# Delta-rule attention and a routed expert layer: other pairs of block inversions, masks and factors multiplied by GpSimd

## The chip, the cores and the metric

The kernel runs on one core of a Trainium2 chip. The metric is device time in microseconds from launch to end. Its engines run beside each other, each with an instruction queue of its own that is worked off in order: PE multiplies matrices, DVE and ACT compute elementwise, POOL (GpSimd) does so more slowly and also starts the indirect transfers, and SP starts most other transfers. SBUF is the on-chip memory; PE writes its results to PSUM, which DVE and ACT can read.

## The reference

Two blocks follow each other. The first is a delta-rule recurrence over 768 tokens, for 4 batches and 8 heads with 48 columns each; the second routes each of the 3072 tokens to 2 of 8 experts with two layers each.

```python
k_n = k / (norm(k) + 1e-6)
for t in range(S):                              # S = 768
    y[t] = q[t] @ state                         # per batch and head, 48 x 48
    v_old = k_n[t] @ state
    state = state + beta[t] * outer(k_n[t], v[t] - v_old)
x = y laid out as (B * S, H * D)                # 3072 x 384

noisy = x @ w_gate + log1p(exp(x @ w_noise)) * noise
top2, weights = the two largest of 8 experts, softmax over them
for each expert e and its tokens:
    out[token] += weight * (relu(x @ w1[e]) @ w2[e])    # 384 -> 1024 -> 384
```

All is in float32.

## The kernel before

**Units and steps.** The recurrence is worked in chunks of 64 tokens. A *unit* is one chunk of two batches (all 8 heads, 128 partitions); there are 12 chunks times 2 pairs of batches, so 24 units. A *step* is two chunks, hence four units; there are 6 steps, 0 to 5, and step s holds units 4s to 4s + 3.

**Products of keys and inversions.** Within a chunk the recurrence is the solution of a triangular system. `products(n)` turns the keys of a unit on PE, multiplies them with each other and copies the blocks of 32x32 into a tile `t` of `inverses`. `invert(g)` inverts all blocks of a group of steps at once on DVE: a transpose, the lengths and factors (with a logarithm and an exponential on ACT), and then 30 columns `j`, each of which is a multiply (line 828) and an add (line 832) that read two operands in SBUF. `GROUPS` says which steps are inverted together: a group of two steps makes each of these 60 operations twice as long. For each step `turn_back` then multiplies the tile with `lower`, a triangle of factors that GpSimd cuts out, and with -1 (line 848), and transposes it twice (lines 855 and 863) to `tb` and `tt`. `INVERTED_AT` and `KEYS_AT` are the places of the tiles.

**Joining and solving.** `join` copies the inverses of 32x32 from `tt` to `w64` on ACT (line 891; eight copies of the last step on DVE) and makes inverses of 64x64 of them with PE products that ACT copies out (lines 925 to 932, with a factor -1 on the way). `recur(n, ...)` is one unit of the recurrence: GpSimd multiplies v with the norms (line 995), PE multiplies keys with queries and with the state, DVE subtracts the second from v (line 1021) and multiplies the first with the causal `mask` (line 1028), PE solves for u, ACT copies u (line 1057), PE adds to the state and ACT copies it (line 1084). `answer` makes y from the masked product `qk`, u and the state; the products with `qk` are issued together with the solve of the following unit where both lie in one group of steps (`PAIRED`), and by themselves at the end of a group.

**Routing.** After steps 1, 3 and 5 `route(g)` takes the two largest experts of the tokens of two steps, counts, and gives each token its two rows in `rows_x`. Sixteen indirect transfers by GpSimd (line 420, called spreads here) write the rows, each held back until PE has reached a certain product, and kept apart by `SPACED` in the plan, save for the last routing. The rows of `rows_x` have to be cleared before (`clear`, `clear_more`): these transfers hang on columns of step 0 and of step 1. `early(1)` and `early(3)` load the first four tiles of expert 0 (line 1406) and work them with the lowest priority.

**Order.** None of this order is that of the text. Each operation is a job with an engine, a cost in us and the data it reads and writes. `Jobs.order` plays through all engines with these costs and picks, among the jobs that can start within `PATIENCE`, the one with the earliest due time. The due times are the constants `BEGINS`, `ENDS`, `ROUTED`, `STORED`; `SOON` pulls in the jobs of a PSUM bank once it is opened, and `COLD` stretches PE's costs by step. The result is written out as it is: every engine's queue has a fixed order.

**Experts.** The rest of expert 0 (line 1888) and the experts 1 to 7 (line 1744) follow, in an order written by hand, with sums of blocks on DVE and GpSimd that save products. Nothing here is touched.

Of the kernel before, what the change touches and what calls it, by code (L numbers as in the profile page):

```python
# [12 lines left out]
ALU = mybir.AluOpType  # L13
# [4 lines left out]
C = 64  # L18
# [6 lines left out]
ROW = 384 + 4  # L25

ROUTES = [(0, 2), (2, 2), (4, 2)]
GROUPS = [(0,), (1, 2), (3, 4), (5,)]
INVERTED_AT = [(0, 0), (1, 0), (0, 0), (1, 0)]
KEYS_AT = [0, 1, 3, 2, 0, 1]  # L30


BEGINS = [1.5, 48.2, 117.9, 200.0]
ENDS = [42.6, 117.5, 132.8, 196.9, 235.5, 240.6]
ROUTED = [146.3, 235.6, 329.3]
STORED = [205.2, 290.3, 366.8]
SOON = 6.93
SPACED = 3.3
COLD = [1.5, 1.35, 1.25, 1.15, 1.1, 1.05]
COLD_KEYS = [1.4, 1.4, 1.3, 1.2, 1.1, 1.1]  # L40

# [56 lines left out]
class Jobs:  # L100
# [145 lines left out]
                    could[jobs[j].engine].add(j)  # L246
        return sorted(done, key=lambda job: job.start)

    PATIENCE = 0.299

    def run(self, link):

# [11 lines left out]
def kernel(  # L264
# [39 lines left out]
    nc = tc.nc  # L304
# [6 lines left out]
    NS = NCH // 2  # L311
    NU = B // 2
    US = 2 * NU
# [17 lines left out]
        out=mask_u, in_=mask_u, pattern=[[1, 128]], base=0, channel_multiplier=-1,  # L331
# [137 lines left out]
    def deltanet(ictx):  # L469
# [5 lines left out]
        jobs = Jobs([psum.tile([128, 2, 512], FP32, name=f"pair{i}") for i in range(3)])  # L475
        p_st = psum.tile([128, 2, 512], FP32, name="p_st")
        PE, ACT, DVE, POOL, SP = Jobs.ENGINES
# [30 lines left out]
        def two_banks(p, cols):  # L508

            return p.tile[:, :, 0 : NP * cols].rearrange("p z (j d) -> p z j d", d=cols)  # L510
# [6 lines left out]
        NQ, N_U = 2 * NU, 3 * NU  # L517
# [207 lines left out]
        def invert(g):  # L725
# [115 lines left out]
            def turn_back(i):  # L841
                s, half = group[i], halves_of[i]
                ends, y, t_key = ENDS[s], inverses[held_in][:, half], ("t", held_in, half)
                if i:
                    only_lower(i)
                jobs.add(
                    DVE, 1.22,
                    lambda y=y: v_.scalar_tensor_tensor(
                        out=y, in0=y, scalar=-1.0, in1=lower, op0=ALU.mult, op1=ALU.mult
                    ),  # L850
                    reads=["lower"], writes=[t_key], due=ends - 4.0,
                )
                jobs.add(
                    DVE, 1.95,
                    lambda y=y: v_.transpose(
                        out=tbs.rearrange("p h j -> p j h"),
                        in_=y.rearrange("p i j -> p j i"),
                    ),
                    reads=[t_key], writes=["tb"], due=ends - 2.0,
                )  # L860
                jobs.add(
                    DVE, 1.95,
                    lambda y=y: v_.transpose(
                        out=tts.rearrange("p h i -> p i h"), in_=y
                    ),
                    reads=[t_key], writes=["tt", ("free", held_in, half)], due=ends,
                )
# [3 lines left out]
        def join(units):  # L871

            pairs = [(slice(lo, lo + Q), slice(lo + Q, lo + 2 * Q)) for lo in (0, C)]

            def part_of(t, n):
                i = n % US
                return t[:, i * H : (i + 1) * H]  # L880

            for n in units:
                w64, tt = w64s(n), part_of(tts, n)
                for lo in range(0, 128, Q):
                    rows, cols = slice(lo, lo + Q), slice(lo % C, lo % C + Q)
                    on, copy = (DVE, nc.vector.tensor_copy) if n >= US * (NS - 1) and lo % C else (
                        ACT, nc.scalar.copy
                    )
                    jobs.add(
                        on, 0.4,  # L890
                        lambda rows=rows, cols=cols, w64=w64, tt=tt, copy=copy: copy(  # L891
                            w64[rows, :, cols], tt[rows]
                        ),
                        reads=["tt"], writes=[("w", n % NW, lo)],
                    )
            for n, m in zip([*units, None], [None, *units]):
                p = bank(1)
                reads = []
                if n is not None:
                    reads += ["tb", ("at", slot_of(n))]  # L900
                if m is not None:
                    reads += [("x", m % 2), *(("w", m % NW, lo) for lo in (Q, C + Q))]

                def p_x(p=p):
                    return p.tile[:, 0 : H * Q].rearrange("p (h i) -> p h i", i=Q)

                def products_of(n=n, m=m, p_x=p_x):
                    for h in range(H):
                        for up, dn in pairs:
                            if n is not None:  # L910
                                matmul(
                                    p_x()[dn, h], ats(n)[up, h % 2, h // 2],
                                    part_of(tbs, n)[up, h], start=(h == 0),
                                    stop=(h == H - 1), skip_group_check=True,
                                )
                            if m is not None:
                                matmul(
                                    p_x()[up, h], xs(m)[dn, h], w64s(m)[dn, h, Q:C],
                                    start=(h == 0), stop=(h == H - 1),
                                    skip_group_check=True,  # L920
                                )

                def negated(n=n, m=m, p_x=p_x):
                    if m is not None:
                        nc.scalar.mul(xs(n), p_x(), -1.0)
                        return
                    for up, dn in pairs:
                        nc.scalar.mul(xs(n)[dn], p_x()[dn], -1.0)

                def joined(m=m, p_x=p_x):  # L930
                    for up, dn in pairs:
                        nc.scalar.copy(w64s(m)[up, :, Q:C], p_x()[up])

                jobs.add(PE, 1.25 if n is not None and m is not None else 0.7, products_of, reads=reads, opens=[p])
                if n is not None:
                    jobs.add(
                        ACT, 0.8 if m is None else 0.47, negated, writes=[("x", n % 2)],
                        **{"closes" if m is None else "uses": p},
                    )
                if m is not None:  # L940
                    jobs.add(ACT, 0.8, joined, writes=[("w", m % NW)], closes=p)
# [39 lines left out]
        def recur(n, m, p_m, p_own):  # L981
# [35 lines left out]
            if c:  # L1017
# [6 lines left out]
                    writes=v_key, uses=p_b,  # L1024
                )
            jobs.add(
                DVE, 0.7,
                lambda: nc.vector.tensor_tensor(
                    out=qks(n), in0=two_banks(p_b, cols)[:, :, :, 0:C],
                    in1=mask[:, None, None, :].to_broadcast([128, 2, NP, C]), op=ALU.mult,  # L1030
                ),
                writes=[("qk", n % NQ)], closes=p_b,
            )
            if p_own:
                add_of_state(n, p_own, True, opens=[p_own], writes=["of_state"])
# [1099 lines left out]
```

## Time and profile before

| | |
|---|---|
| median of 3 runs | 808.8 us (805.58 to 812.17) |
| profiled execution | 808.39 us, of which span 806.7 us |
| PE busy, mean granted clock | 697.7 us, 0.922 |
| DVE busy | 555.2 us |
| ACT busy | 302.5 us |
| POOL busy | 365.7 us |

The span runs from the first to the last instruction of the profiled execution, and all times of the trace count from its start. The granted clock is the share of TensorE's full clock that the chip allowed. An engine's busy time says nothing on whether the others wait for it; the rows below show that by stretch and by instruction.

### The profile page before, as it was taken

What the parts mean: (1) busy time and instruction counts of PE and PEld (TensorE: products, weight loads), DVE (VectorE), ACT (ScalarE), POOL (GpSimd) and SP (SyncE); (2) the same over time, 40 slices, a digit from 0 to 9 for tenths busy, and PEclk for the clock granted to TensorE, in tenths of its full rate; (3) what the DMA queues carried; (4) which work ended last, traced back from release to release, by engine and by line L of the source; (5) the groups of instructions that cost most, each with busy time, mean ns of one, the idle gap of its engine ahead of it and who ended that gap; (6) DMA issues with size and microseconds to landing.
All of it is one profiled execution on the core that took longest, in us unless ns stands there. A gap on an engine that the chain in (4) does not pass through costs nothing.

```text
span 806.7 us, 20922 instructions
## 1 busy us (share of the span) xinstructions
PE 697.7 (86%) x8734; PEld 532.2 (66%) x8734; DVE 555.2 (69%) x1128; ACT 302.5 (37%) x702; POOL 365.7 (45%) x376
## 2 busy tenths in 40 slices
PE   3666568777778878689999999999999999999995
PEld 3556557566667655456569679578588587597593
DVE  5968787996788221085488598597696796796751
ACT  2768287655664431112340430430520521511500
POOL 2101101102433334607366784884884875785411
PEclk8755867997789999989999999999999999999998
DMA  3769873636334212854406406407408309201201
GB/s 56 141 113 337 186 212 67 169 74 180 84 87 108 82 72 84 305 109 133 137 21 176 146 20 187 149 5 195 144 1 231 105 3 271 68 20 43 61 31 34
DMA packets 142215, 93.69 MB, mean 116 GB/s; under 512 B 115865, under 2 KB 134588, under 8 KB 141088
## 3 DMA queue, kind: packets, MB, share of 16 engines
q1 hardware_dynamic: 130448, 64.54, 31.2%
q0 software_dynamic: 9552, 27.33, 10.1%
q8 instruction: 70, 1.15, 0.6%
q10 hardware_dynamic: 2112, 0.39, 0.3%
q14 instruction: 33, 0.27, 0.1%
HBM read 58.82 MB, written 34.81 MB: 116 GB/s over the span
## 4 chain that ended last, share of the span: by engine, by line
PE 66%; ACT 10%; issue 9%; DVE 5%; SPq 4%; POOL 2%; DMA 2%; another core or an unknown queue 1%; POOLq 0%; ACTq 0%; DVEq 0%
PE inner L1744 26%; PE outer L1744 16%; PE pair L481 11%; PE pair L484 3%; PE pair L1483 3%; SPq L616 2%; PE pair L1460 2%; PE inner L1867 2%; ACT w L891 2%; DMA kp<-in_k_dram 2%; PE inner L1888 2%; DVE part L828 1%; ACT t L712 1%; DVE t L832 1%; PE outer L1900 1%
## 5 line engine op out<-in xcount | busy, mean ns | idle before, releaser
L1827 ACT ACTIVATE hT<-inner 128x416 f32<-128x416 f32 x105 | 54.3, 517 | 256.8 <-PE inner L1744 249.1
L1821 DVE TENSOR_TENSOR hT<-hT,inner 128x416 f32<-128x416 f32 x182 | 105.1, 586 | 45.4 <-PE inner L1744 34.4
L463 POOL DMA_INDIRECT out_dram<-sums,index x52 | 53.1, 1021 | 113.6 <-DVE sums L1647 98.0
L420 POOL DMA_INDIRECT rows_x<-y,slot x48 | 48.4, 1009 | 82.8 <-PE pair L481 32.8
L1744 PE MATMUL inner<-s_x,w1e 128*128 128x416 f32 x196 | 78.7, 512 | 0.0
L1647 DVE SCALAR_TENSOR_TENSOR sums<-outer,gate,sums 128x192 f32<-128x192 f32 (+1 forms) x113 | 45.7, 414 | 35.8 <-PE outer L1744 33.6
L1816 ACT ACTIVATE hT<-hT 128x416 f32<-128x416 f32 x112 | 60.7, 548 | 21.8 <-DVE hT L1821 13.8
L995 POOL TENSOR_TENSOR v<-v,norms 128x384 f32<-128x384 f32 x24 | 21.6, 901 | 97.4 <-DMA v<-in_v_dram 50.7
L454 POOL DMA_INDIRECT sums<-out_dram,index x49 | 51.8, 1057 | 19.0 <-issue 11.1
L832 DVE TENSOR_TENSOR t<-t,part 128x168 f32<-128x168 f32 (+28 forms) x120 | 55.7, 464 | 4.1
L1744 PE MATMUL outer<-t_w,hT 128*128 128x192 f32 x336 | 58.1, 326 | 0.0
L828 DVE TENSOR_TENSOR part<-t 128x168 f32<-128x168 f32 (+28 forms) x120 | 55.4, 461 | 3.5
L1744 PEld LDWEIGHTS inner<-s_x,w1e 128*128 128x128 f32 x196 | 37.0, 190 | 31.5 <-issue 27.7
L1744 PE MATMUL inner<-s_x,s_w 128*128 128x416 f32 x140 | 56.9, 512 | 0.0
L1744 PE MATMUL inner<-xe,w1e 128*128 128x416 f32 x140 | 55.8, 513 | 0.0
L1744 PEld LDWEIGHTS outer<-t_w,hT 128*128 128x128 f32 x336 | 55.1, 190 | 0.1
L1701 POOL TENSOR_TENSOR w1e<-w1e 128x256 f32<-128x256 f32 x54 | 51.4, 962 | 2.0
L1744 PE MATMUL outer<-w2e,hT 128*128 128x192 f32 x280 | 50.1, 326 | 0.0
L1744 PEld LDWEIGHTS outer<-w2e,hT 128*128 128x128 f32 x280 | 46.5, 190 | 2.2 <-issue 2.2
L1744 PEld LDWEIGHTS inner<-s_x,s_w 128*128 128x128 f32 x140 | 26.5, 190 | 22.4 <-issue 22.2
L1744 PE MATMUL outer<-t_w,s_h 128*128 128x192 f32 x224 | 40.6, 329 | 0.0
L787 POOL TENSOR_SCALAR_AFFINE_SELECT lower<-factor 128x1024 f32<-128x1024 f32 x6 | 10.7, 1784 | 64.3 <-DVE factor L764 50.3
(226 smaller groups left out, 1530.3 us busy)
## 6 DMA issues: line engine op xcount, KB each, us to landing
w2e<-in_moe_w_dram SPq DMA_DIRECT2D x8, 1536.0 KB
w1e<-in_moe_w_dram SPq DMA_DIRECT2D x8, 1536.0 KB
xq<-rows_x SPq DMA_DIRECT2D x28, 312.0 KB
rows_x<-empty SPq DMA_DIRECT2D x8, 776.0 KB
qp<-in_q_dram SPq DMA_DIRECT2D x48, 96.0 KB
v<-in_v_dram SPq DMA_DIRECT2D x48, 96.0 KB
out_dram<-empty SPq DMA_DIRECT2D x4, 1152.0 KB
rows_x<-empty SPq DMA_DIRECT2D x8, 485.0 KB
```

Of the source, the lines that this page charges most:

```text
L420: d = nc.gpsimd.indirect_dma_start(out=rows_x, out_offset=bass.IndirectOffsetOnAxis(ap=slot, axis=0), in_=rows, in_offset=None,).ins
L454: nc.gpsimd.indirect_dma_start(out=got, out_offset=None, in_=out, in_offset=bass.IndirectOffsetOnAxis(ap=index, axis=0), bounds_check=N - ...
L463: nc.gpsimd.indirect_dma_start(out=out, out_offset=bass.IndirectOffsetOnAxis(ap=index, axis=0), in_=got, in_offset=None, bounds_check=N - ...
L481: latest[0] = nc.tensor.matmul(*x, **y).ins
L828: v_.tensor_tensor(out=part, in0=factor.to_broadcast(shape), in1=row.to_broadcast(shape), op=ALU.mult,)
L832: v_.tensor_tensor(out=block, in0=block, in1=part, op=ALU.add)
L1647: nc.vector.scalar_tensor_tensor(out=got, in0=p, scalar=gate, in1=got, op0=ALU.mult, op1=ALU.add)
L1701: engine.tensor_tensor(out=block(to), in0=block(x), in1=block(y), op=ALU.add if sign == "+" else ALU.subtract,)
L1744: nc.tensor.matmul(p, lhsT, rhs, start=opens and i == 0, stop=i == len(products) - 1, skip_group_check=True,)
L1816: nc.scalar.activation(h, h, ACTF.Relu)
L1821: nc.vector.tensor_tensor(out=h, in0=h, in1=p, op=ALU.add if sign > 0 else ALU.subtract)
L1827: nc.scalar.mul(h, p, float(sign))
```

## The change

Steps 0 and 1 are now inverted by themselves, 2 together with 3 and 4 together with 5. [...] The causal mask is applied by GpSimd too; since that engine can't read PSUM, ACT first copies the product to SBUF. The due times and `COLD` have other values, and with them and the jobs the order of all engines up to the experts is planned anew.

```diff
-GROUPS = [(0,), (1, 2), (3, 4), (5,)]
-INVERTED_AT = [(0, 0), (1, 0), (0, 0), (1, 0)]
+GROUPS = [(0,), (1,), (2, 3), (4, 5)]
+INVERTED_AT = [(0, 0), (0, 1), (1, 0), (0, 0)]
-BEGINS = [1.5, 48.2, 117.9, 200.0]
-ENDS = [42.6, 117.5, 132.8, 196.9, 235.5, 240.6]
-ROUTED = [146.3, 235.6, 329.3]
-STORED = [205.2, 290.3, 366.8]
-SOON = 6.93
+BEGINS = [2.4, 43.3, 71.4, 173.4]
+ENDS = [42.2, 92.1, 142, 181.5, 247.6, 278.9]
+ROUTED = [129.0, 258.2, 283.6]
+STORED = [190.4, 253.8, 339.8]
+SOON = 2.39
-COLD = [1.5, 1.35, 1.25, 1.15, 1.1, 1.05]
-COLD_KEYS = [1.4, 1.4, 1.3, 1.2, 1.1, 1.1]
+COLD = [1.5, 1.35, 1.3, 1.25, 1.25, 1.2]
+COLD_KEYS = [1.4, 1.4, 1.35, 1.3, 1.25, 1.25]
-    PATIENCE = 0.299
+    PATIENCE = 0.132
...
-                    DVE, 1.22,
-                    lambda y=y: v_.scalar_tensor_tensor(
-                        out=y, in0=y, scalar=-1.0, in1=lower, op0=ALU.mult, op1=ALU.mult
-                    ),
+                    POOL, 2.4,
+                    lambda y=y: [nc.gpsimd.tensor_tensor(out=y, in0=y, in1=lower, op=ALU.mult)],
...
-                    on, copy = (DVE, nc.vector.tensor_copy) if n >= US * (NS - 1) and lo % C else (
-                        ACT, nc.scalar.copy
+                    on, times = (
+                        (DVE, nc.vector.tensor_scalar_mul) if n >= US * (NS - 1) and lo % C
+                        else (ACT, nc.scalar.mul)
                     )
...
-                        lambda rows=rows, cols=cols, w64=w64, tt=tt, copy=copy: copy(
-                            w64[rows, :, cols], tt[rows]
+                        lambda rows=rows, cols=cols, w64=w64, tt=tt, times=times: times(
+                            w64[rows, :, cols], tt[rows], -1.0
...
-                        nc.scalar.mul(xs(n), p_x(), -1.0)
+                        nc.scalar.copy(xs(n), p_x())
...
-                        nc.scalar.mul(xs(n)[dn], p_x()[dn], -1.0)
+                        nc.scalar.copy(xs(n)[dn], p_x()[dn])
...
-                DVE, 0.7,
-                lambda: nc.vector.tensor_tensor(
-                    out=qks(n), in0=two_banks(p_b, cols)[:, :, :, 0:C],
+                ACT, 0.6, lambda: nc.scalar.copy(qks(n), two_banks(p_b, cols)[:, :, :, 0:C]),
+                writes=[("qk", n % NQ)], closes=p_b,
+            )
+            jobs.add(
+                POOL, 1.2,
+                lambda: [nc.gpsimd.tensor_tensor(
+                    out=qks(n), in0=qks(n),
                     in1=mask[:, None, None, :].to_broadcast([128, 2, NP, C]), op=ALU.mult,
-                ),
-                writes=[("qk", n % NQ)], closes=p_b,
+                )],
+                writes=[("qk", n % NQ)],
```

## Rows read from the trace of the kernel before

**Rows 1.** Stretches: PE, PEld, DVE, ACT, POOL busy us, clock, DMA share, GB/s.

```profile
115.20:186.50 71.30, 53.05 (x1823) 45.23 (x1824) 61.46 (x123) 46.37 (x119) 9.28 (x9) 0.84 0.44 115
186.50:252.40 65.90, 51.30 (x1770) 43.41 (x1768) 50.08 (x117) 42.17 (x106) 23.52 (x25) 0.85 0.43 112
...
362.80:806.70 443.90, 433.86 (x1947) 320.59 (x1945) 318.16 (x565) 116.72 (x226) 275.40 (x258) 0.99 0.33 99
```

**Rows 2.** DVE's timeline (start, duration): last transpose of each inverted step.

```profile
48.40 1.90 DVE L863 STREAM_TRANSPOSE tt<-t 128x1024 f32<-128x1024 f32 x1
...
113.43 1.87 DVE L863 STREAM_TRANSPOSE tt<-t 128x1024 f32<-128x1024 f32 x1
...
132.16 1.94 DVE L863 STREAM_TRANSPOSE tt<-t 128x1024 f32<-128x1024 f32 x1
...
184.62 1.90 DVE L863 STREAM_TRANSPOSE tt<-t 128x1024 f32<-128x1024 f32 x1
...
210.11 1.96 DVE L863 STREAM_TRANSPOSE tt<-t 128x1024 f32<-128x1024 f32 x1
...
250.56 1.95 DVE L863 STREAM_TRANSPOSE tt<-t 128x1024 f32<-128x1024 f32 x1
```

**Rows 3.** Timeline of ACT, copies of solved units 7, 8, 12, 15 and 23.

```profile
145.72 0.48 ACT L1057 COPY u<-pair 128x384 f32<-128x384 f32 x1
...
147.85 0.48 ACT L1057 COPY u<-pair 128x384 f32<-128x384 f32 x1 [0.85 <-PE pair L481]
...
198.44 0.48 ACT L1057 COPY u<-pair 128x384 f32<-128x384 f32 x1
...
227.16 0.48 ACT L1057 COPY u<-pair 128x384 f32<-128x384 f32 x1 [0.49 <-PE pair L484]
...
290.21 0.48 ACT L1057 COPY u<-pair 128x384 f32<-128x384 f32 x1 [1.75 <-PE pair L484]
```

**Rows 4.** Timelines of SP and PE: early rows' loads, expert 0's rest.

```profile
259.67 1.72 SPq L1406 DMA_DIRECT2D kp<-rows_x  x2
...
321.09 0.81 SPq L1406 DMA_DIRECT2D kp<-rows_x  x2
...
362.82 3.39 PE L1888 MATMUL inner<-xe_r,w1e 128*128 128x320 f32 x12
```

**Rows 5.** Groups by line: busy us, mean ns | idle us before.

```profile
L1028 DVE TENSOR_TENSOR qk<-pair,mask 128x512 f32<-128x512 f32 x24 | 16.3, 680 | 0.0
...
L648 ACT COPY qs<-pair 128x512 f32<-128x512 f32 x24 | 14.0, 590 | 11.6 <-PE pair L484 10.3 <-PE pair L481 0.9
...
L848 DVE SCALAR_TENSOR_TENSOR t<-t,lower 128x1024 f32<-128x1024 f32 x6 | 7.3, 1214 | 0.2
...
L420 POOL DMA_INDIRECT rows_x<-y,slot x48 | 48.4, 1009 | 82.8 <-PE pair L481 32.8
```

**Rows 6.** GpSimd's products by tile and line: count, ns min/median/max.

```profile
L995 POOL TENSOR_TENSOR v<-v,norms x24: 822/836/1267, 33.4 to 266.9; 128x384 f32<-128x384 f32 x24
...
L1717 POOL TENSOR_TENSOR t_w<-w2e x14: 1805/1832/2151, 365.1 to 743.9; 128x768 f32<-128x768 f32 x14
```

**Rows 7.** Timeline of all engines beside a GpSimd product.

```profile
33.27 0.41 DVE L832 TENSOR_TENSOR t<-t,part 128x238 f32<-128x238 f32 x1
33.35 1.02 POOL L995 TENSOR_TENSOR v<-v,norms 128x384 f32<-128x384 f32 x1 [12.24 <-DVE part L828]
...
33.72 0.91 DVE L828 TENSOR_TENSOR part<-t 128x234 f32<-128x234 f32 x1
```

**Rows 8.** Timeline of DVE, where inversions begin, and one stall.

```profile
14.24 1.25 DVE L769 STREAM_TRANSPOSE t<-t 128x1024 f32<-128x1024 f32 x1
...
62.46 0.55 DVE L752 RECIPROCAL length<-root 128x64 f32<-128x64 f32 x1 [8.81 <-ACT root L747]
...
87.12 0.55 DVE L1021 TENSOR_TENSOR v<-v,pair 128x384 f32<-128x384 f32 x1 [4.83 <-DMA kp<-in_k_dram]
...
125.22 0.55 DVE L752 RECIPROCAL length<-root 128x64 f32<-128x64 f32 x1 [6.63 <-ACT root L747]
```

More of the change, by code (lines that the diff above doesn't have):

```diff
@@ L921, in products_of, with moved_on @@
                                 )
-                def negated(n=n, m=m, p_x=p_x):
+                def moved_on(n=n, m=m, p_x=p_x):
                     if m is not None:
-                        nc.scalar.mul(xs(n), p_x(), -1.0)
+                        nc.scalar.copy(xs(n), p_x())
                         return
                     for up, dn in pairs:
-                        nc.scalar.mul(xs(n)[dn], p_x()[dn], -1.0)
+                        nc.scalar.copy(xs(n)[dn], p_x()[dn])
                 def joined(m=m, p_x=p_x):
@@ L936, in join @@
                     jobs.add(
-                        ACT, 0.8 if m is None else 0.47, negated, writes=[("x", n % 2)],
+                        ACT, 0.8 if m is None else 0.47, moved_on, writes=[("x", n % 2)],
                         **{"closes" if m is None else "uses": p},
```

## Prediction

> **What bounds the kernel now.** I read the table by stretch first [rows 1]. The last stretch, 443.9 us of expert products, has PE busy for 433.86 us at a granted clock of 0.99; its instructions are the same after the change, so I carry it over as it is. The profiled execution took 808.39 us, which is these 443.9, the 362.8 us before them and 1.7 us around the span. The median of the three runs is 808.8 us, 0.05% from it, so the sum is made on 808.4. All that can move is the time at which expert 0's remaining rows enter PE, now 362.82 us [rows 4].
>
> Before that, no single engine is full. From 115.2 to 186.5 us DVE is busy for 61.46 of 71.3 us, PE for 53.05 and ACT for 46.37 [rows 1]: DVE comes nearest. So the second view is the six transposes that end an inversion, one per step [rows 2]: steps 0 to 5 become usable at 50.3, 115.3, 134.1, 186.5, 212.1 and 252.5 us. The third is the copies of solved units [rows 3]: unit 7 (last of step 1) at 145.72, unit 8 at 147.85, 12 at 198.44, 15 (last of step 3) at 227.16, 23 (last of all) at 290.21. From 12 to 23 a unit takes 91.8/11 = 8.3 us, from 8 to 23 142.4/15 = 9.5 us, the wait for step 3 included. Thus the inversions set the pace to about 190 us, and the recurrence itself from there.
>
> The fourth view is the end [rows 4]. The early rows of tiles 2 and 3 are loaded at 321.09 us, when route 1's spreads (steps 2 and 3) have landed; PE needs 362.82 - 321.09 = 41.7 us from there to expert 0's rest. That load is 93.9 us behind unit 15's solve: y, logits, route 1 and sixteen paced spreads lie between.
>
> **The masks.** A mask on DVE costs 0.68 us, 24 times, 16.3 us in all [rows 5]; it reads one operand from PSUM. Afterwards ACT copies the product out, 24 times the 0.59 us that a copy of 128x512 takes [rows 5]: 14.2 us more on ACT, which has 24.9 us idle in 115.2 to 186.5 and 23.7 in 186.5 to 252.4 [rows 1]. I cost that at nothing while these gaps cover it; where one falls in front of a solved unit's copy, it costs 0.59 us per unit.
>
> GpSimd then multiplies. No row shows 128x512, so I go from its nearest products [rows 6]: 0.836 us for 384 elements, 1.832 for 768, hence 2.59 ns an element: 1.17 us for 512 and 2.50 us for 1024 (estimates). GpSimd has time for 24 x 1.17 = 28 us: it is busy for 9.28 of 71.3 us.
>
> But the engines get in each other's way. A v product of 384 elements starts at 33.35 us; the column operation that DVE starts at 33.72 takes 0.91 us, where the one of the larger form at 33.27 takes 0.41 [rows 7]. So 0.5 us of DVE is lost per GpSimd product that meets a column. For 512 elements I scale by duration: 0.5 x 1.17/0.83 = 0.7 us, taken as 0.75; the ends are 0 (it meets a transpose or an operation on PSUM) and 1.17 (all of it). The Trainium skill speaks against the change here: SBUF — State Buffer, "Who interferes with whom", says that a DVE instruction with two SBUF inputs and a GpSimd instruction that reads SBUF exclude each other, and that the second one blocks fully. By that rule a mask on GpSimd would take 1.17 us from the columns where it took 0.68 before; the row shows the block, but only 0.5 us of the 0.83. So the mask gives DVE nothing where it meets a column, and 0.68 us where it doesn't.
>
> **The factors.** Six multiplies of 1.21 us leave DVE [rows 5] and take 2.50 us on GpSimd, with the two transposes of the same step waiting for them. DVE hides 1.25 us of one by transposing the next group's diagonals [rows 8]; behind the last group nothing does. I charge 1.3 us per inversion. The minus sign moves into copies of the inverses that are made anyway, now with a factor; I cost that at nothing, either way.
>
> **The regrouping, step by step.** Two single and two double inversions remain, so DVE's column work is equal; only the order differs.
> - Step 0: 50.3 + 1.3 = 51.6 us.
> - Step 1: a whole single inversion took 50.3 - 14.2 = 36.1 us [rows 2, 8]. The new one can begin under step 0's multiply, near 45.3 (50.3 less a multiply and two transposes, 5.0): 45.3 + 36.1 + 1.3 (waiting for that multiply) + 3.8 (step 0's transposes) + 1.3 + 1.1 (two subtractions on v at 0.55 [rows 8]) + 4 x 0.75 (masks of step 0) = 92 us, 23 earlier than now.
> - Step 2: a double inversion from its first reciprocal to the end took 115.3 - 62.5 = 52.8 us [rows 2, 8]. Less 4 masks (2.7), plus 1.3, two more subtractions (1.1) and 6 x 0.75: 57 us. It holds a stall of 4.83 us in front of a subtraction [rows 8], of which I keep half: 92 + 57 - 2.4 = 146.5 us, 12 later than now.
> - Step 3 follows its partner by 18.8 to 25.6 us [rows 2]: 165 to 172, some 18 earlier.
> - Step 4: the second double took 186.5 - 125.2 = 61.3 us with route 0 in it. Less 8 x 0.68, plus 1.3 and 8 x 0.75: 63 us. 146.5 + 63 = 210, where it is now. Step 5: 229 to 235, some 20 earlier.
>
> Units follow. Unit 8 now comes 13.8 us behind step 2's readiness; then 160. Seven units at 9.0 us, between the two paces above, put unit 15 at 223.3 (now 227.2), eight more at 8.3 put unit 23 at 289 (now 290). The recurrence ends where it did: what the regrouping gives to steps 1, 3 and 5 it takes from step 2.
>
> **Where a gain is left: the tail.** Route 1 gains 3.9 us from unit 15, and 5.1 more because its DVE work now has step 5's multiply and two transposes in its way (1.21 + 2 x 1.95 us [rows 2, 5]), which will lie before it. The load goes out at 312.1 us instead of 321.1. PE must be done with tiles 0 and 1 by then, 9 us sooner than now. Their rows are loaded at 259.67 us [rows 4]; unit 7, now 30.4 us behind step 1, comes at 122, so this load moves by 23 us to 237. From there to 289 PE has 22% idle (51.30 of 65.9 us busy [rows 1]), 11 us for these products: enough. SP issues both loads in order behind those of q and v for later units; I cost that at nothing, as these are wanted sooner than the rows, and at one unit's 8 us at worst. So the rest enters PE at 312.1 + 41.7 = 353.8 instead of 362.8: 353.8 + 443.9 + 1.7 = 799 us. If the cover for tiles 0 and 1 is gone, 808.
>
> **The rivals.**
> - More: no mask meets a column and the recurrence goes at 8.3 us from unit 8 on. Step 2 at 142, unit 8 at 156, unit 15 at 214, 13 us earlier; with the 5 us of route 1 the rest enters at 345: 790 us, and 780 if each of the 15 units behind unit 8 is also 0.68 us shorter, the mask being out of DVE's queue. For it: DVE also has transposes, routing and reads of PSUM that a mask could meet. Against it: a double inversion is mostly columns, and most units are solved beside one.
> - Nothing: each mask costs the columns 1.17 us. Fourteen of them at 0.42 us more than I took put step 4 at 215 and step 5 behind it, so that its transposes meet route 1 as now, and unit 15 near 226: 808 us. The Trainium skill's rule in its full form gives this time.
> - Slower: GpSimd as a queue. 48 spreads stand in it, before which it idles for 82.8 us, mostly for PE [rows 5], 1.7 us each, and each takes 1.0. A mask behind a spread makes the next unit's solve wait, and the queue is refilled by PE: a loop. The price is 1.7 + 1.0 us for each unit that is hit; six of units 8 to 23 make 16 us on today's time: 824 us. It decides from the point at which a masked product is ready later than the unit's copy on ACT. Against it: the product is wanted one unit later, 8 us.
>
> **How the numbers follow.** Forecast 799 (791 to 808 within its bounds: masks 0 to 1.17 us, pace 8.3 to 9.5, cover or none), chance 0.40; more, 0.22; nothing, 0.20; slower, 0.18. A change of 1%, 8 us, is about what three runs that lie 0.8% apart can tell. Below 800 lie 0.24 of the forecast's chance, all 0.22 of "more" and 0.04 of "nothing": faster 0.50; above 816 lies "slower" and 0.01 of the others: 0.19; the same 0.31. The range reaches to the far end of "more" and to four of the six hits of "slower", which leaves some 0.15 out: 779 to 820.
>
> **What would show it.** The ends of the six transposes near 52, 92, 146, 168, 210 and 232 us; unit 15 near 223 and unit 23 near 289; masks of about 1.2 us with stretched columns beside them; the load of the early rows near 312 and the rest's first product near 354; the expert stage unchanged at 443.9. Wrong would make it: another pace of the units; GpSimd waiting in front of masks; clears of the token rows, which hang on step 1's columns and so go out 23 us earlier, in the way of k and v; or a route 1 that the new due times put elsewhere, from which I read no time.

## Result and the profile after

The changed kernel takes 812.93 us in the median of 19 runs, the kernel before 808.8 in as many beside it: a ratio of 1.0058, with a 95% interval of 1.0031 to 1.0085. It is 0.6% slower, inside the range, on the other side of no change than the 799 us forecast. The ratio leaves out runs more than 1.5% above the fastest of their kernel, four of the changed kernel's 19. The profiled execution has a span of 808.8 us where before had 806.7.

The first view of the profile after is the table by stretch (columns as in [rows 1]):

```profile
115.20:186.50 71.30, 52.89 (x1636) 46.24 (x1636) 61.14 (x115) 51.86 (x135) 26.93 (x21) 0.77 0.40 107
186.50:252.40 65.90, 48.78 (x1666) 41.59 (x1666) 49.13 (x81) 39.28 (x96) 35.91 (x34) 0.86 0.53 149
364.90:808.80 443.90, 433.66 (x1947) 320.75 (x1945) 319.60 (x568) 116.73 (x226) 275.43 (x258) 0.99 0.34 100
```

The expert stage is 443.9 us long again. But DVE, from which masks and factors were taken, is busy for as long as before in the two stretches (61.14 and 49.13 us against 61.46 and 50.08), and GpSimd for 30 us more. Next, DVE's timeline with the last transpose of each step, as in [rows 2]:

```profile
52.00 1.90 DVE L861 STREAM_TRANSPOSE tt<-t 128x1024 f32<-128x1024 f32 x1
...
98.62 1.97 DVE L861 STREAM_TRANSPOSE tt<-t 128x1024 f32<-128x1024 f32 x1
...
143.73 1.94 DVE L861 STREAM_TRANSPOSE tt<-t 128x1024 f32<-128x1024 f32 x1
...
170.82 1.96 DVE L861 STREAM_TRANSPOSE tt<-t 128x1024 f32<-128x1024 f32 x1 [0.24 <-ACT w L890]
...
225.12 1.96 DVE L861 STREAM_TRANSPOSE tt<-t 128x1024 f32<-128x1024 f32 x1
...
246.60 1.97 DVE L861 STREAM_TRANSPOSE tt<-t 128x1024 f32<-128x1024 f32 x1
```

Steps 0 to 5 are ready at 53.9, 100.6, 145.7, 172.8, 227.1 and 248.6 us. Step 4, forecast for 210, is 17 us late, and the copies of solved units 8, 15, 16 and 23 on ACT (as in [rows 3]) show who waits for it:

```profile
165.49 0.48 ACT L1060 COPY u<-pair 128x384 f32<-128x384 f32 x1 [0.56 <-PE pair L481]
...
222.77 0.48 ACT L1060 COPY u<-pair 128x384 f32<-128x384 f32 x1 [1.32 <-PE pair L484]
...
238.36 0.48 ACT L1060 COPY u<-pair 128x384 f32<-128x384 f32 x1
...
294.63 0.48 ACT L1060 COPY u<-pair 128x384 f32<-128x384 f32 x1 [0.64 <-PE pair L484]
```

Unit 8 comes at 165.5, 5 us behind the forecast, and unit 15 at 222.8 as forecast; then there are 15.6 us to unit 16, the first of step 4, and unit 23 comes 4.4 us later than before. The gap was made where the second double inversion begins, on DVE:

```profile
149.53 1.24 DVE L769 STREAM_TRANSPOSE t<-t 128x1024 f32<-128x1024 f32 x1
155.16 1.25 DVE L769 STREAM_TRANSPOSE t<-t 128x1024 f32<-128x1024 f32 x1 [4.40 <-ACT t L712]
...
160.69 0.55 DVE L752 RECIPROCAL length<-root 128x64 f32<-128x64 f32 x1
...
168.24 0.20 DVE L828 TENSOR_TENSOR part<-t 128x60 f32<-128x60 f32 x1
```

From step 2's readiness to the first reciprocal pass 15.0 us, and to the first column 22.6: route 0's work lies there, a wait for ACT's copies of step 5's key products, and step 3's transposes. And the columns themselves are slower. Three groups by line (as in [rows 5]; line 848 is the multiply with `lower`, now on GpSimd) and DVE's and GpSimd's timeline at two masks:

```profile
L1031 POOL TENSOR_TENSOR qk<-qk,mask 128x512 f32<-128x512 f32 x24 | 35.6, 1486 | 50.5 <-ACT qk L1026 50.2
...
L848 POOL TENSOR_TENSOR t<-t,lower 128x1024 f32<-128x1024 f32 x6 | 14.2, 2366 | 13.3 <-DVE r_w L1212 7.5 <-DVE t L839 5.7
L1026 ACT COPY qk<-pair 128x512 f32<-128x512 f32 x24 | 14.0, 588 | 8.7 <-DVE v L1020 8.3 <-PE pair L481 0.4
```

```profile
181.41 1.25 POOL L420 DMA_INDIRECT rows_x<-y,slot  x1 [0.16 <-issue]
...
181.80 0.57 DVE L828 TENSOR_TENSOR part<-t 128x396 f32<-128x396 f32 x1
182.41 1.99 DVE L832 TENSOR_TENSOR t<-t,part 128x396 f32<-128x396 f32 x1
182.69 1.27 POOL L1031 TENSOR_TENSOR qk<-qk,mask 128x512 f32<-128x512 f32 x1
...
200.35 0.66 DVE L832 TENSOR_TENSOR t<-t,part 128x476 f32<-128x476 f32 x1
200.44 1.71 POOL L1031 TENSOR_TENSOR qk<-qk,mask 128x512 f32<-128x512 f32 x1 [0.64 <-ACT qk L1026]
201.04 1.60 DVE L828 TENSOR_TENSOR part<-t 128x468 f32<-128x468 f32 x1
```

A column operation that takes 0.57 us takes 1.99 beside a mask that follows a spread, and one that is a little smaller than one of 0.66 takes 1.60 beside a mask alone. Summed over the trace to 300 us (each duration less the shortest of its line and shape), the columns lose 23.5 us where they lost 11.7 before, of which 23.1 and 11.1 in operations that overlap an instruction of GpSimd. Eight columns that waited for a mask with no spread right ahead of it lost 0.84 to 1.06 us, 0.96 in the median; two that waited for a mask right behind a spread lost 1.29 and 1.42, and one that met a spread, a v product and a mask in a row 2.53. A column that waits for a v product alone loses 0.51 in the median, and 18 that overlapped only a spread lost 0.1 in sum.

The last view is the end, on SP and PE, as in [rows 4]:

```profile
297.09 0.51 PE L1437 MATMUL pair<-ident,kp 128*128 128x128 f32 x3
...
322.89 0.80 SPq L1409 DMA_DIRECT2D kp<-rows_x  x2
...
325.54 4.78 PE L1486 MATMUL pair<-w2e,t 128*128 128x384 f32 x14 [0.67 <-ACT kp L1500]
330.16 0.85 PE L1437 MATMUL pair<-ident,kp 128*128 128x128 f32 x6
...
364.87 3.39 PE L1891 MATMUL inner<-xe_r,w1e 128*128 128x320 f32 x12
```

PE begins tiles 0 and 1 at 297.1, behind the last unit, and is done with them at 330.2; only then does it turn the rows of tiles 2 and 3, whose load was issued at 322.9. The load doesn't release PE; PE comes to it from its own queue. It was so before the change: DVE read the rows that had landed at 323.5, while PE was at tiles 0 and 1 from 294 to 326.6.

```profile
294.05 0.51 PE L1434 MATMUL pair<-ident,kp 128*128 128x128 f32 x3
...
323.51 0.15 DVE L1423 CAST early_index<-kp 128x1 int32<-128x1 f32 x1 [11.69 <-DMA kp<-rows_x]
...
326.56 0.50 PE L1434 MATMUL pair<-ident,kp 128*128 128x128 f32 x3
```

### The profile page after: what moved, and what is told of

Its sections match the earlier page's. It is cut to its first block, busy times and chain, and to the rows that moved or that the text cites. A ratio compares the mean times of both kernels' runs of the same rounds, so it can differ in the third digit from the quotient of the medians.

```text
span 808.8 us, 20949 instructions
## 1 busy us (share of the span) xinstructions
PE 698.8 (86%) x8734; PEld 536.2 (66%) x8734; DVE 552.2 (68%) x1098; ACT 314.8 (39%) x726; POOL 412.9 (51%) x406
## 4 chain that ended last, share of the span: by engine, by line
PE 65%; issue 10%; DVE 8%; ACT 7%; SPq 5%; POOL 3%; DMA 1%; POOLq 0%; DVEq 0%; ACTq 0%
PE inner L1747 26%; PE outer L1747 16%; PE pair L481 10%; DVE part L828 3%; SPq L616 3%; PE pair L1463 3%; DVE t L832 3%; PE pair L1486 3%; PE pair L484 2%; PE inner L1870 2%; PE inner L1891 2%; PE outer L1903 1%; SPq L602 1%; ACT w L890 1%; POOL out_dram L463 1%
## 5 line engine op out<-in xcount | busy, mean ns | idle before, releaser
L828 DVE TENSOR_TENSOR part<-t 128x168 f32<-128x168 f32 (+28 forms) x120 | 62.5, 521 | 3.7
L832 DVE TENSOR_TENSOR t<-t,part 128x168 f32<-128x168 f32 (+28 forms) x120 | 60.5, 504 | 4.1
L1031 POOL TENSOR_TENSOR qk<-qk,mask 128x512 f32<-128x512 f32 x24 | 35.6, 1486 | 50.5 <-ACT qk L1026 50.2
L481 PE MATMUL pair<-v,w 64*64 64x48 f32 x768 | 36.7, 251 | 9.6 <-issue 7.7
```

The lines of the kernel that those rows point to most:

```text
L481: latest[0] = nc.tensor.matmul(*x, **y).ins
L828: v_.tensor_tensor(out=part, in0=factor.to_broadcast(shape), in1=row.to_broadcast(shape), op=ALU.mult,)
L832: v_.tensor_tensor(out=block, in0=block, in1=part, op=ALU.add)
```

## Experiments

They ran on three other chips (e1 to e4, e5 to e8, e9 to e16), on which the kernel before takes some 1.3% less (797.3 to 798.4 us), so each is given by its ratio to before beside it, on the same chip; the changed kernel itself ran again on the second of them (e5). "Rest" is the first product of expert 0's rest.

| | ratio (95%) | step 4 ready | unit 23 | rest |
|---|---|---|---|---|
| e1 mask sliver | 0.9989 (0.9954 to 1.0023) | 218.5 | 285.2 | 349.7 |
| e2 mask twice | 1.0220 (1.0175 to 1.0266) | 236.3 | 304.0 | 368.5 |
| e3 regroup, planned anew | 1.0182 (1.0142 to 1.0222) | 229.1 | 294.3 | 362.7 |
| e4 offload, planned anew | 1.0172 (1.0135 to 1.0209) | 222.0 | 300.7 | 367.2 |
| e5 changed kernel | 1.0067 (1.0029 to 1.0104) | 227.0 | 291.6 | 356.1 |
| e6 unpaced | 1.0137 (1.0096 to 1.0178) | 224.7 | 299.6 | 365.6 |
| e7 early cut | 1.0043 (1.0014 to 1.0072) | 222.7 | 293.4 | 355.3 |
| e8 cut, unpaced | 1.0090 (1.0062 to 1.0119) | 229.3 | 298.4 | 359.8 |
| e9 mask on DVE | 1.0024 (0.9994 to 1.0055) | 222.6 | 291.2 | 355.8 |
| e10 factor on DVE | 1.0059 (1.0025 to 1.0092) | 224.3 | 294.8 | 360.9 |
| e11 both on DVE | 1.0018 (0.9986 to 1.0049) | 221.1 | 291.3 | 355.9 |
| e12 before, mask on GpSimd | 1.0055 (1.0028 to 1.0082) | 212.5 | 287.4 | 355.6 |
| e13 before, SOON 6.0 | 1.0003 (0.9964 to 1.0042) | 212.8 | 285.2 | 354.4 |
| e14 changed, SOON 2.6 | 1.0280 (1.0231 to 1.0329) | 238.2 | 307.2 | 371.3 |
| e15 late masks on GpSimd | 1.0016 (0.9986 to 1.0046) | 222.1 | 288.7 | 353.1 |
| e16 before, early between | 1.0202 (1.0145 to 1.0259) | 216.6 | 319.1 | 369.3 |

The last three columns are us of the one profiled execution, which strays from the median by up to 4 us (e10 lies 4 above it).

**How much a mask costs.** e1 and e2 change only the size of GpSimd's job.

```diff
-                    out=qks(n), in0=qks(n),
-                    in1=mask[:, None, None, :].to_broadcast([128, 2, NP, C]), op=ALU.mult,
-                )],
+                    out=qks(n)[:, :, :, 0:4], in0=qks(n)[:, :, :, 0:4],     # e1
+                    in1=mask[:, None, None, 0:4].to_broadcast([128, 2, NP, 4]), op=ALU.mult,
+                ) for _ in range(2)],       # e2: the whole multiply, for _ in range(2)
```

> The changed kernel in its own order on every engine, but GpSimd multiplies only 4 of the 64 columns of each head with the causal mask (most of the mask is left out). Theory 'lock' (GpSimd's mask holds DVE's columns, 0.9 us each by the trace, some 14 of them before step 5 is ready): step 4 is ready 10 to 13 us before 227, the hole between units 15 and 16 goes, unit 23 comes at 284 to 287 and the time falls by 7 to 10 us, to 803 to 806. Rival 'regrouping' (step 4 is late since its inversion begins late and meets ACT's and route 0's work): step 4 moves by under 3 us and the time by under 2 us, 811 to 814.

> The changed kernel in its own order on every engine, but GpSimd applies the causal mask twice, one multiply right behind the other (the product is the same, as the mask holds ones and zeros). Lock: each doubled mask takes another 0.9 us from the columns, step 4 comes 11 to 13 us later, and the time grows by 10 to 18 us, to 823 to 831. Rival (the masks stand beside slack): under 3 us more, 811 to 816.

Against e5 the sliver is 0.8% faster, 6 us, and the doubled mask 1.5% slower, 12 us. Step 4, unit 23 and the rest move together, by 17.8, 18.8 and 18.8 us from e1 to e2. The first came out a little under its expectation (step 4 8.5 us sooner than in e5, where 10 to 13 were expected, and the hole between units 15 and 16 stays, 14.6 us in both), the second within it in time, with step 4 9.3 us later for the 11 to 13 expected; "slack" is refuted.

**Which part it is, planned anew.** e3 has before's code with the new groups and constants, e4 the new code with before's groups and constants.

```diff
-GROUPS = [(0,), (1, 2), (3, 4), (5,)]
+GROUPS = [(0,), (1,), (2, 3), (4, 5)]     # e3, with the other constants; e4 the reverse
```

> The kernel before with the new groups and planning constants alone; masks and factors stay on DVE and the order is planned with them there. Lock: the regrouping is sound and the offload spoils it. With 0.68 us of DVE per mask in place of 0.9 to 1.3 and the factor at 1.21 in place of 2.5, step 4 is ready at 215 to 220 and the time is 802 to 807, below the kernel before. Rival 'regrouping': the order 1+1+2+2 itself makes step 4 late; step 4 at 224 to 230 and 811 to 816.

> The changed code with the groups and planning constants of before: masks and factors on GpSimd, steps 1 with 2 and 3 with 4. Lock: DVE gains nothing per mask and each of the four inversions ends 1.3 us later by the factor; steps 3 and 4 come 2 to 6 us behind 186.5 and 212, and the time is 810 to 816. Rival 'regrouping': the offload frees DVE, step 3 is ready 4 to 8 us before 186.5 and the time is 800 to 806.

Both are 1.7 to 1.8% slower than before, and so 1% slower than the two parts together, and slower than either of their two expectations, which end at 816 us, 1.009 of before. Step 4 came at 229 in e3, where the rival had it, and at 222 in e4, 10 us late where 2 to 6 were expected. But two parts that cost 1.7% each can't make 0.6%: these are other plans, not parts of the one at hand, and they settle nothing by themselves.

**Which part it is, in one plan.** So e9 to e12 leave the plan alone: the planner sees the job as before, and only the engine that executes it is another (the lines that take the instruction out of GpSimd's queue or into it are left out here).

```diff
-                lambda: [nc.gpsimd.tensor_tensor(        # e9, e11: mask
+                lambda: [nc.vector.tensor_tensor(
...
-                    lambda y=y: [nc.gpsimd.tensor_tensor(out=y, in0=y, in1=lower, op=ALU.mult)],
+                    lambda y=y: [v_.scalar_tensor_tensor(        # e10, e11: factor
+                        out=y, in0=y, scalar=1.0, in1=lower, op0=ALU.mult, op1=ALU.mult
...
-                lambda: nc.vector.tensor_tensor(        # e12, in the kernel before
-                    out=qks(n), in0=two_banks(p_b, cols)[:, :, :, 0:C],
+                lambda: (nc.scalar.copy(qks(n), two_banks(p_b, cols)[:, :, :, 0:C]),
+                nc.gpsimd.tensor_tensor(
+                    out=qks(n), in0=qks(n),
```

> The changed kernel with its plan as it is, PE, ACT and SP in the same order; only the causal mask is multiplied by DVE instead of GpSimd, at the place that the plan gives it (ACT still copies the product out first). Lock: a mask then costs DVE 0.6 to 0.7 us where GpSimd's took 0.9 to 1.3 from the columns; the columns of steps 4 and 5 take 32 to 35 us instead of 40.8, step 4 is ready 2 to 5 us sooner and the time is 2 to 5 us below the changed kernel's (1.001 to 1.004 of before). Rival (the mask on GpSimd is free): step 4 comes 4 to 6 us later by 8 masks, and the time is 4 to 8 us more.

> The changed kernel with its plan as it is; only the multiply with the factors' triangle is done by DVE (1.2 us) instead of GpSimd (2.35 us), at the same place. If the path runs through the inversions: step 0 2 to 4 us sooner (DVE waited 4.15 us for that multiply), step 4 2 to 4 us sooner, and the time 2 to 4 us less. Rival (the waiting DVE had nothing else that was late): under 1 us.

> Both of the last two: in the changed kernel's plan masks and factors are multiplied by DVE, so that the regrouping is left alone. Lock: 4 to 8 us less than the changed kernel, 0.997 to 1.002 of before; the regrouping by itself is then worth nothing either way. Rival 'regrouping' (pairs 2 with 3 and 4 with 5 cost the 5 us): as the changed kernel, 1.005 to 1.009.

> The kernel before with its plan as it is; only the causal mask is done as after the change, a copy by ACT and a multiply by GpSimd, in the place where DVE multiplied. Lock: each mask beside columns costs them 0.9 to 1.3 us where DVE took 0.68; 10 to 14 such masks ahead of step 5, so the time is 2 to 6 us more than before (1.003 to 1.008). Rival (the offload frees DVE): 3 to 8 us less, 0.990 to 0.996.

With the mask back on DVE 3.4 us of the changed kernel's 5.3 are gone; with the factor too, 3.9, and what is left can't be told from before. The 5.3 us are e5's, from another chip, and the intervals of e5 and e9 overlap; on one chip e10, with its masks on GpSimd, takes 2.8 us more than e9 and 3.7 more than e11 (means, 95%: 2.8 us either way). In before's own plan the mask's move, ACT's copy included, costs 0.55%. e9, e11 and e12 took as long as expected. The factor's move costs nothing that can be measured, although step 0 comes 5 us and step 4 some 3 us sooner without it: here the rival was right, with under 1 us. How DVE's columns of steps 4 and 5 change is read from the two lines 828 and 832 in the stretch of these columns (busy us and count, clock, DMA share, GB/s), first in the changed kernel:

```profile
168.20:220.70 52.50, 20.49 (x30) 0.75 0.63 187
...
168.20:220.70 52.50, 20.36 (x30) 0.75 0.63 187
```

and with the mask on DVE (e9):

```profile
168.50:215.90 47.40, 15.16 (x30) 0.73 0.68 201
...
168.50:215.90 47.40, 16.78 (x30) 0.73 0.68 201
```

The same 60 operations take 40.85 us or 31.94: 8.9 us less, 1.5 for each of the six masks in that stretch (not eight, as expected; four of them directly follow another instruction of GpSimd), where a mask on DVE cost 0.68 [rows 5] and from the copy in SBUF costs 0.68 in the median, 0.85 in the mean (e9: the mean holds those that met another product of GpSimd).

**Columns or the unit's own chain.** e15 is e9 with the masks of units 16 to 23, behind the columns, left on GpSimd.

```diff
+                lambda: [(nc.vector if n < 4 * US else nc.gpsimd).tensor_tensor(
```

> The changed kernel's plan with the masks of units 0 to 15 on DVE and those of units 16 to 23, behind nearly all columns, on GpSimd. If the columns are what a mask costs: as with all masks on DVE, 1.001 to 1.004 of before. Rival (GpSimd's 1.3 us in each unit's own chain costs): between that and the changed kernel, 1.004 to 1.006.

It is as fast as e9: the mask costs where columns run, and GpSimd's longer time in a unit's chain costs nothing that these runs can tell.

**What sets the tail.** e6 takes the pacing from route 1's spreads, e7 leaves out products of tiles 0 and 1, e8 does both.

```diff
-                            latest[0] if paced else None,
+                            latest[0] if paced and g == 0 else None,       # e6, e8
...
+                        if s == 1 and f0 not in (0, FT - 1):       # e7, e8, in back()
+                            return
```

> The changed kernel in its own order, but route 1's sixteen spreads are no longer held back until PE has reached a certain product. The last two of them waited 10.8 us for that. Theory 'PE sets the tail' (from unit 23 to the rest PE has 68 us of early products, none of them done before): the load of tiles 2 and 3 goes out 6 to 11 us sooner, the rest enters PE within 2 us of where it was, and the time is within 2 us of the changed kernel's. Rival (the prediction's tail: the rest follows that load by 41.7 us): the time falls with the load, by 6 to 11 us.

> The changed kernel in its own order, but tiles 0 and 1 of expert 0 leave out 6 of the 8 parts of the second layer's sum (24 of 32 matmuls of 0.34 us each, about 8 us of PE). PE sets the tail: the products of tiles 2 and 3 begin sooner, but no sooner than their rows land, near 325 where they began at 330.2, so 4 to 6 us less. Rival (the load alone sets it): within 1 us of the changed kernel.

> Both of the last two: 6 of 8 parts of tiles 0 and 1's second layer left out, and route 1's spreads not held back. PE sets the tail: with the rows there in time, all of the 8 us of products is gained, 7 to 9 us less than the changed kernel. Rival (the load sets it): as much as without the pacing alone.

e6 failed both theories: it is 0.7% slower than e5, and the load went out at 328.6 us, not sooner. Its GpSimd and PE timelines say why:

```profile
275.59 0.96 POOL L420 DMA_INDIRECT rows_x<-y,slot  x1 [0.30 <-issue]
276.58 1.27 POOL L1031 TENSOR_TENSOR qk<-qk,mask 128x512 f32<-128x512 f32 x1
...
277.90 0.34 PE L481 MATMUL pair<-u,qk 64*64 64x48 f32 x2 [3.92 <-POOL qk L1031]
...
319.28 0.33 POOL L1329 COPY y<-meta 128x16 f32<-128x16 f32 x2 [21.68 <-DVE meta L1200]
320.05 0.98 POOL L420 DMA_INDIRECT rows_x<-y,slot  x1 [0.44 <-issue]
```

Eleven spreads went out back to back, the mask behind them came at 276.6 where e5 has it at 268.6, and PE waited 3.92 us for it: the forecast's rival "GpSimd as a queue", which the pacing had kept away. And route 1's last spread stands behind a copy that waits for route 2, so in this order no pacing could have let it go earlier. In e7 PE waits for the rows instead; its two lines, and then those of e5:

```profile
324.15 1.22 PE L1437 MATMUL pair<-ident,kp 128*128 128x128 f32 x6 [2.76 <-DMA kp<-rows_x]
326.10 2.07 PE L1463 MATMUL pair<-kT,w1e 128*128 128x256 f32 x4 [0.73 <-ACT kT L1449]
...
327.14 0.84 PE L1437 MATMUL pair<-ident,kp 128*128 128x128 f32 x6
328.97 1.13 PE L1463 MATMUL pair<-kT,w1e 128*128 128x256 f32 x4 [0.99 <-ACT kT L1449]
```

Tiles 2 and 3 begin 3.0 us sooner than in e5, though unit 23 came 1.8 later: 4.8 of the 8 us, until the load is what ends last. But the rest entered PE only 0.8 us sooner, and the time fell by 0.24%, within the noise, where 4 to 6 us were expected. Part of the 2.2 us lost again goes with the granted clock, which fell behind that wait, as the stretch of 324 to 330 us has it (columns as in [rows 1]):

```profile
324.00:330.00 6.00, 4.63 (x15) 3.34 (x15) 0.76 (x6) 1.96 (x8) 3.66 (x4) 0.72 0.92 292
```

The first four products took 2.07 us where e5 has 1.13 for them. So PE sets the tail; in e5 DVE read the landed rows at 322.4, 4.7 us before PE turned them, and 3.0 before the change. e8 against e6 (-0.5%) says the same, though e8 too missed its expectation: with unpaced spreads it isn't faster than e5.

**The gaps.** e16 puts the products of tiles 0 and 1 between the last units of the kernel before.

```diff
+        between = [j for j in jobs if j.late is not None and j.late < 1 and j.engine <= self.ACT]
+        for x, j in enumerate(j for j in between if j.engine == self.PE):
+            ready[j.number] = 246.0 + 1.1 * x
+        for j in between:
+            j.key = 0, 0.0
```

> The kernel before, planned so that the 42 groups of products for tiles 0 and 1 of expert 0 come one every 1.1 us from 246 us on, between the last units, instead of behind the last one. PE sets the tail and has gaps there: unit 23 comes 10 to 22 us later, tiles 2 and 3 begin with the load of their rows, and the time is 0 to 8 us less than before (0.990 to 1.000). Rival (each product delays the recurrence by all that it takes, 22 us or more): the same or up to 10 us more, 1.000 to 1.012.

Units 20 to 23 on ACT:

```profile
280.51 0.48 ACT L1062 COPY u<-pair 128x384 f32<-128x384 f32 x1 [5.53 <-PE pair L1465]
...
285.46 0.48 ACT L1062 COPY u<-pair 128x384 f32<-128x384 f32 x1 [0.79 <-PE pair L1465]
...
309.26 0.48 ACT L1062 COPY u<-pair 128x384 f32<-128x384 f32 x1 [2.17 <-PE pair L1488]
...
319.14 0.48 ACT L1062 COPY u<-pair 128x384 f32<-128x384 f32 x1 [5.02 <-PE pair L1488]
```

Unit 23 comes 34 us later than in e13, whose plan is nearly before's, and the time is 2% more, beyond the rival's bound. The idle fifth of PE is no room for products at these places; whether better places exist wasn't tried.

**The plan.** One constant turned a little, in either kernel:

```diff
-SOON = 6.93
+SOON = 6.0      # e13, in before; e14, in the changed kernel: 2.6 for 2.39
```

> The kernel before with one planning constant turned a little, SOON 6.0 in place of 6.93; the work is the same, and the planned order differs in some places. If the plan alone is worth a per cent or more: 1.004 to 1.015 of before. Rival (the order matters little, and what was planned anew was slow for its parts): 0.998 to 1.003.

> The changed kernel with SOON 2.6 in place of 2.39, again the same work in another planned order. Plan: 4 us or more away from the changed kernel (over 1.011 or under 1.002 of before). Rival: within 0.3% of it.

Before doesn't feel it; the changed kernel loses 2.1% with the same work, step 4 ready 11 us later. That is over three times what the whole change costs, and more than the 1% by which e3 and e4 lie above it. None of the versions beats the kernel before. Where e11 makes up for its late step 4 is seen in the stretch from unit 23 to the rest (columns as in [rows 1]), in e11 and then in e13:

```profile
291.30:355.90 64.60, 53.43 (x286) 35.27 (x286) 17.20 (x68) 13.88 (x43) 24.75 (x28) 1.00 0.53 162
...
285.20:354.40 69.20, 57.20 (x286) 37.66 (x287) 20.59 (x74) 13.92 (x43) 26.68 (x29) 0.95 0.50 155
```

## Why the prediction was wrong

Two steps carry the miss: the gain of 9 us was placed in the tail, which didn't work as assumed (third point), and the loss of some 4 us is the masks' (first point).

- **"The mask gives DVE nothing where it meets a column" (0.75 us each).** The step that failed by sign. In the stretch of steps 4 and 5 a mask takes 1.5 us from the columns, in the mean; alone it takes about 0.96, and right behind a spread 1.3 to 1.4. So where it meets a column DVE loses 0.3 to 0.8 us by the move instead of breaking even. The slip is the scaling by duration: a v product of 0.83 us costs a column 0.51 and a mask of 1.27 costs 0.96, both 0.3 less than they last, so the price grows by all that the longer product adds. The end of 1.17 us was nearer, and e9, e11 and e12, with e1 and e2 for the direction, show that this is the slowdown: 0.4 to 0.55% in either plan. The Trainium skill's rule (SBUF — State Buffer, "Who interferes with whom") is nearer to this than the value taken: the trace agrees that the two exclude each other, at 0.96 of the mask's 1.27 us when it is alone, and at more than the whole of it behind a spread. The estimate of 1.17 us for the mask itself was sound (1.27 alone).
- **"Step 4: 146.5 + 63 = 210".** An error of reckoning: 61.3 us was counted from the first reciprocal, and then added to step 2's readiness. Between the two lay 9.9 us in before [rows 2, 8]; after, 15.0. With 9.9 the sum gives 219; e11, with masks and factors on DVE, has 221.1, and on GpSimd they bring it to 227. Step 5, counted from step 4, is 17 us late with it (248.6). So the regrouping makes step 4 late by itself, and what it gives to steps 1, 3 and 5 it takes from 2 and 4, not from 2 alone. e11 against before shows no gain or loss from it that can be measured (groups and new order together, which no run here separates), though unit 23 comes 6.1 us later in e11 than in e13, whose plan is nearly before's: the rest comes only 1.5 us later. The tail between them is 4.6 us shorter in e11, at a granted clock of 1.00 against 0.95; how much of this the new order brings, and how much the single execution, isn't shown.
- **"The load to the rest: 41.7 us" and the covered products.** The gain of 9 us was to come from here, and the step was wrong in before already: PE began tiles 0 and 1 at 294 us and was done at 326.6, behind the load at 321, whose rows DVE read at 323.5. The chain was unit 23, then PE's own queue. In e1, e2, e5, e9, e11 and e15, with the clock granted in full in that stretch, the rest follows unit 23 by 64.5 or 64.6 us; in e6 and e10, at 0.97, by 66.0 and 66.2. In the first comparison it is 72.6 before and 70.2 after: there PE also stood still once for 4.2 and 4.7 us, near 340 us, behind an idle ACT, and the profile names no instruction of this kernel that ended ACT's idle time. The idle 22% were no cover (e16): they were put at 11 us and called enough, while the products of tiles 0 and 1 keep PE busy for 24.5 us in before's trace, a cost that the sum didn't have.
- **Route 1, 9 us sooner.** Unit 15 was (222.8), the load wasn't (322.9 against 321.1): the route's DVE work ended at 260.1 us as before, its 15th spread then waited 10.8 us for PE, until 314.8, and its last is queued behind a copy that waits for route 2 (e6).
- **Factors, 1.3 us per inversion.** DVE waited 4.15 us for GpSimd at step 0 and 2.46 at step 4, more than charged, but in the time nothing of it can be seen (e10).
- **Right:** steps 0 and 3 within 5 us, the first early load (240.7 for 237), the mask's and factor's own time on GpSimd (2.50 forecast, 2.37 measured), the expert stage. ACT's 24 copies were put at nothing; no run takes them out, so up to the 0.2% that e11 keeps may be theirs, or nothing.
- **Right by luck:** step 2 and unit 15. Step 1 came 8.6 us late, and step 2's inversion took 66.6 us from its first reciprocal for the 57 forecast, but that reciprocal ran at 79.1, 21.5 us before step 1 was ready. Unit 8 came 5 us late, and the units behind it went at 8.2 us each, faster than the 9.0 taken and than both bounds (8.3 and 9.5).

The outcome is the rival "nothing" in its price for a mask and in the missing gain of the tail, with step 4 12 us later than it had, and slower instead of equal. That the 12 us make this difference isn't shown: step 4 comes at 221 in e11, which can't be told from before.

## What to carry to other kernels

Work moved from DVE to GpSimd isn't free for DVE while DVE reads two SBUF operands: set nearly the other engine's whole duration (0.96 of 1.27 us here, and more right behind a spread) against what DVE saves, and move only what runs beside no such work. Before a gain is placed in a chain, ask for each link what ended its wait: a load that landed before its reader was free is no link, and an inversion's count must begin where the last one ended. In a kernel whose order is planned, judge a part by exchanging the engine within one plan, since another plan alone moved the time by 2%.

## What was not expected of the hardware

- A column operation beside a mask that directly follows an indirect transfer's issue on GpSimd lost 1.4 us (1.99 against 0.57), more than the mask lasts (1.27), though columns beside a spread alone lose nothing. A v product right behind a spread cost 1.36 (before, 208.1 us) where one by itself costs 0.51. Why isn't shown. The hindrance goes both ways: that engine's mask takes 1.27 us alone and up to 3.3 beside DVE, 1.49 in the mean.
- Behind a wait of PE of 2.76 us, before which it had been busy for 2.47 of 6 us, the granted clock was 0.72 over the next 6 us (e7), so that the wait cost more than its length: the first four products lost 0.94 of the 3.0 us that had been won.
